# New orders for an attention-plus-MLP kernel, with fewer dummy matmuls in its first batch

One core of one Trainium2 chip. The metric is device time of one execution in microseconds (us), the slowest core's; here there is one. Dies and slow dies do not matter.

## The reference

Nyström attention on 8 batches of 8 heads, 576 tokens, head dimension 64, with 32 landmarks, followed by an MLP with squared ReLU.

```python
A  = sm(q, k_lm); Bm = sm(q_lm, k_lm); C = sm(q_lm, k)     # sm: scaled scores, softmax
Z  = Bm.T / (norm1(Bm) * norminf(Bm) + 1e-6)
for _ in range(6):
    Z = 2 * Z - Z @ Bm @ Z                                  # Newton steps, 32x32 per head
attn = A @ Z @ C @ v
h = x @ w_in; r = max(h, 0); out = (r * r) @ w_out          # x: [4608, 512], d_ff 2048
```

## The kernel before

Each batch runs as named steps. A written list says in which order they are issued: HEAD for batch 0's attention, then one list per batch, which mixes that batch's MLP (`h`: four matmuls of 288 columns and a relu; `s`: the square) with the next batch's attention and with output matmuls (a number n: n matmuls of 512 columns). Each engine follows the list in order; it waits only where its next instruction's inputs are missing.

```python
HEAD = (
    "w:16 ck tk1 mk w:1:256 w:1:256 ek1d w:1:256 w:1 tk0 tt w:1 w:1 cq0 cq1 ek0a mq tq0 tq1 "
    # ... cut ...
    "jl at:0 ea0d ea1a ct w:1:256 nu w:1:256 g:0 gl1d fv w:1 gf1d w:1 gf0a az gl0d"
)
```

`w:n:width` is n dummy matmuls, which keep TensorE busy and compute nothing:

```python
def warm(n, width=512):
    z = bds[1].rearrange("p a b c -> p (a b c)")
    for _ in range(n):
        nc.tensor.matmul(idle[:, 0:width], lhsT=z[:, 0:P], rhs=z[:, 0:width], start=True, stop=True)
```

The other steps of the head that matter here: `ck`, `cq0`, `cq1` reorder k and the two halves of q as they arrive; `tk`, `tq` transpose on TensorE and `ek`, `eq` copy the result out (last letter: `d` VectorE, `a` ScalarE); `mk`, `mq` are the segment means; `ls`, `ib`, `if` lead to EY, the start of the inverse; `jo` is one joint Newton step (four in all), `jl`, `nu`, `fv` the last ones; `sum`, `rec`, `row` normalise the score rows of A on VectorE; `cv`, `cr` are C times v and C's column sums; `az` gives AZ, after which the MLP of batch 0 can begin.

```python
def joint_step(old, diagonal):
    nv = products(diagonal, lambda qd: ...)           # 8 matmuls of 32x32 blocks on TensorE
    new = newt.tile([P, 2, 2, M], BF16, tag="EY", name="EY")
    last = twice_less(new, old, nv)                   # one VectorE instruction: 2*old - nv
    return new, stationary(new[:, :, 0, :], "ED"), last
```

The softmax here doesn't subtract the row's maximum and nothing guards it: scores larger than these inputs give would overflow.

Of the kernel before, what the change touches and what calls it, by code (L numbers as in the profile page):

```python
# [9 lines left out]
P = 128  # L10
# [23 lines left out]
DMA_C = 9  # L34
COMPACT = 1
HEAD = (
    "w:16 ck tk1 mk w:1:256 w:1:256 ek1d w:1:256 w:1 tk0 tt w:1 w:1 cq0 cq1 ek0a mq tq0 tq1 "
    "lm w:1 et w:1:256 w:1 eq0a w:1:256 tl eq1d ls sum:0:4:5 w:1 ib w:1 w:1:256 sq1 w:1:256 "
    "if sk1 sum:1:2:5 w:1:256 w:1 sum:1:0:2 jo w:1:256 w:1:256 rec:1 w:1:256 row:1:0:3 "
    "row:1:3:5 w:1:256 sk0 w:1 sq0 jo w:1:256 w:1:256 w:1 w:1:256 sum:0:2:4 sum:0:0:2 w:1 jo "  # L40
    "rec:0 cv:0 cv:1 w:1:256 w:1:256 row:0:3:5 cr jo w:1:256 row:0:0:3 w:1:256 at:1 cba w:1 "
    "jl at:0 ea0d ea1a ct w:1:256 nu w:1:256 g:0 gl1d fv w:1 gf1d w:1 gf0a az gl0d"
)
LOADS = "w10 v0 w00 q1 w01 w11 o0 o1 o2 o3 v1"
PLANS = [
    (
        "pk h g:1 tt h pq h s tk1 s h s h tq1 s tk0 h h mk s s mq tq0 h lm s g:2 g:3 ls sk0 s h "
        "h ib 1 h 1 s if tl h jo 1 sq0 s 1 jo s s 1 h jo 1 sq1 1 jl h 1 nu h s s h nn 2 sk1 nu s "
        "1 s 8 as0 1 ar0 as1 2 ar1 5 nn1 cv 4 wt at0 2 gg0 2 at1 2 gg1 1"
    ),  # L50
    (
        "2 pk 1 h h 1 mk pq s mq 1 s h tq0 lm h ls h tt tq1 3 tl 1 s 1 h ib 1 s if s sq1 2 s h "
        "jo 1 as1 sq0 1 h h s 1 as0 tk1 1 jo 1 s 4 tk0 2 jo 1 h 1 s h 1 pk+ 1 jl ar1 h sk0 1 s 1 "
        "s nu h s 1 sk1 s h h nn s cv nu h 3 nn1 at1 s 3 s wt 3 ar0 2 gg0 3 at0 1 gg1 pq+"
    ),
    (
        "5 mk h 1 h mq s 2 h 5 lm s 2 ls 1 sk1 2 ib 3 h h s sk0 s if 1 s h 2 h 1 jo s h tl 3 jo "
        "1 s 2 h jo 1 s 2 h 3 s sq0 s 1 jl pk+ 4 sq1 2 as0 nu 3 h 1 nn 2 as1 1 pq+ 1 nu 1 h 1 "
        "ar1 h 1 s s h 1 nn1 cv 1 h 2 ar0 1 s wt h 1 at0 2 gg1 1 s at1 1 s 2 gg0 1 s"
    ),  # L60
    (
        "mk 2 h 1 mq 7 h 2 s lm s 1 ls 1 h sq1 1 h h 1 ib 1 s if sk1 1 s h s 2 h jo 1 s 1 h s 1 "
        "jo 2 h 1 pk+ jo 1 tl s h 2 jl as1 sq0 1 s h 1 s h nu s 1 h sk0 s 1 ar1 4 as0 nn 1 ar0 2 "
        "h 3 cv 2 s h nu 4 s nn1 1 at1 1 h wt 2 s 3 s gg1 1 at0 4 gg0 4 pq+"
    ),
    (
        "2 mk h 2 mq 4 h lm 1 h 1 s ls 1 sk0 s ib s 3 h h if 3 tl s 2 h h s 1 s jo 2 h h 1 jo s "
        "1 sq0 s 2 h 1 jo 5 s 10 jl pk+ s 3 sq1 h nu 1 h 1 h 3 as0 sk1 s 1 h 1 as1 ar1 5 s nn cv "
        "nu pq+ 4 s 2 nn1 ar0 h s 4 wt h 2 at0 s 1 gg0 2 s 1 at1 1 gg1 2"
    ),  # L70
    (
        "3 mk mq 3 h lm 3 h h ls 1 s 1 s ib 2 sq1 h 2 if 1 sq0 3 jo h 1 sk0 s jo 2 s h jo tl 4 "
        "as1 1 h 1 jl s sk1 h 3 pk+ s 4 nu h 1 s 2 s 1 s 4 as0 h 1 ar1 nn s 2 ar0 h cv h nu h s "
        "1 s 1 nn1 h 2 h pq+ s wt h 2 at1 2 gg0 at0 5 s 3 s s gg1"
    ),
    (
        "mk 1 mq 3 h s lm 1 h 3 ls 2 h s 1 ib 2 h 1 if sq1 s h 1 s 3 sq0 2 s h 2 s 2 jo h tl 3 "
        "jo 1 h h as0 jo 3 s h 1 s jl 1 s sk1 4 nu 2 as1 h nn 1 h 1 sk0 2 ar0 nu 1 s s 3 h h 1 "
        "cv 2 nn1 s h s 1 at0 1 wt h 2 s 1 ar1 gg0 1 at1 2 s 1 gg1 4 s"
    ),  # L80
    (
        "h 7 h 6 s 1 h 6 h 1 s 2 h s 2 h 6 s 13 h 2 s 2 h 1 s 1 s 5 s h 3 h 1 s s h 11 s 1 h s 8 "
        "h 1 h 1 h 1 s 4 s h 2 s s"
    ),
]

# [2 lines left out]
def kernel(  # L89
# [9 lines left out]
    nc = tc.nc  # L99
# [27 lines left out]
        nc.vector.memzero(ect[:])  # L127
        ects.append(ect)

    behind, gate = [], []  # L130

    def load(dst, src, queue=nc.gpsimd):
        with tc.issue_after(behind[0].ins) if behind else nullcontext():
            d = queue.dma_start(dst, src)  # L134
        if gate:
            tc.add_manual_dep(
                d.ins, gate.pop().ins.name,
                mybir.DependencyInfo(mybir.DependencyClass.Sync, mybir.DependencyReason.DATA),
                reason="q first")
        if queue is nc.gpsimd:  # L140
            behind[:] = [d]
        return d

    def k_row(b):
        return TAIL if b % 2 == 0 else 0

    def q_row(b):
        return TAIL - k_row(b)
# [12 lines left out]
    def load_qk(b: int, X: dict):  # L161

        X["qkt"] = loads.tile([P, H, D], BF16, tag="qkt", name="qkt")

        def tails():
            for src, r0 in ((k, k_row(b)), (q, q_row(b))):
                load(X["qkt"][r0:r0 + TAIL, :, :],
                     src[b, :, NC4 * P:S, :].rearrange("h p d -> p h d"))

        if b > 0:  # L170
            tails()
        for nm, src in (("k", k), ("q", q)):
            if b < 3:
                X[nm + "raw"] = staged(b, nm)
            else:
                X[nm + "raw"] = loads.tile([P, H, NC4, D], BF16, tag="raw", name="raw")
            parts = ((0, H // 2), (H // 2, H)) if b == 0 and nm == "q" else ((0, H),)
            for lo, hi in parts:
                one = load(
                    X[nm + "raw"][:, lo:hi, :, :],  # L180
                    src[b, lo:hi, 0:NC4 * P, :].rearrange("h (p c) d -> p h c d", c=NC4),
                    nc.sync if b == 0 and nm == "k" else nc.gpsimd)
                if b > 0 and nm + "turn" in loaded[b - 1]:
                    tc.add_manual_dep(
                        one.ins, loaded[b - 1][nm + "turn"].ins.name,
                        mybir.DependencyInfo(mybir.DependencyClass.Sync,
                                             mybir.DependencyReason.DATA),
                        reason="behind the turning of the batch before")
            if b == 0 and nm == "k":
                tails()  # L190

# [9 lines left out]

    loaded = {b: {} for b in range(B)}
    load_qk(0, loaded[0])

    def band(t, pattern, base, mult):
# [28 lines left out]
    for i in range(2):  # L234
        ct = const.tile([P, 2, NC4 + 1, P], BF16, name="ct%d" % i)
# [1 line left out]
        cts.append(ct)  # L237
    nc.vector.tensor_copy(seg[:, NC4 + 2, :], seg[:, NC4, :])

    def load_rest(after):  # L240

        def w_in(i, j):
            load(
                w_in_bf[64 * i:64 * i + 64, :, 1024 * j:1024 * j + 1024],
                moe_w_in[256 * i:256 * i + 256, 1024 * j:1024 * j + 1024].rearrange(
                    "(j d) f -> d j f", d=D),
            )

        def w_out(j):
            load(  # L250
                w_out_bf[:, 4 * j:4 * j + 4, :],
                moe_w_out[512 * j:512 * j + 512, :].rearrange("(ft fp) c -> fp ft c", fp=P),
            )

        behind[:] = [masked]
        for x in LOADS.split():
            i = int(x[1])
            if x[0] == "w":
                w_in(i, int(x[2]))
            elif x[0] == "o":  # L260
                w_out(i)
            else:
                (load_v if x[0] == "v" else load_qk)(i, loaded[i])

    turn = [0]
# [32 lines left out]
    def attention(b: int, R: dict):  # L298

        X = loaded[b]  # L300
        BD = bds[b % 2]
        ect = ects[b % 2]
        first = b == 0
# [193 lines left out]
        ct = cts[b % 2] if b >= DMA_C else None  # L497
        c0 = b % 2
        at = NC4 * (1 - c0)
# [10 lines left out]
        an = attn.tile([P, 2, NC4 + 1, P], BF16, tag="an", bufs=1, name="an")  # L510
        AT = attn.tile([P, 2, (NC4 + 1) * P], BF16, tag="AT", name="AT")
# [55 lines left out]
        one, two = slice(0, 1), slice(1, 2)  # L567
# [20 lines left out]

        def a_transposed(i):
            if b >= DMA_A:  # L590
                nc.sync.dma_start_transpose(AT[:, i, :].rearrange("p (c t) -> p c t", t=P),
                                            an[:, i, :, :].rearrange("p c x -> p (c x)"))
                return
            tps = ntile([P, (NC4 + 1) * P], BF16, placed=b > 0)
            for c in range(NC4 + 1):
                nc.tensor.transpose(tps[:, c * P:c * P + P], an[:, i, c, :], ident_bf[:])  # L596
            o = TAIL * c0
            return AT[:, i, o:o + S], tps[:, o:o + S]
# [42 lines left out]
        act, dve = nc.scalar.copy, nc.vector.tensor_copy  # L641
# [67 lines left out]
        def head_step(token):  # L709
            st = X["state"]  # L710
            name, *args = token.split(":")
            i = int(name[2]) if len(name) > 2 and name[2].isdigit() else 0
            n = [int(x) for x in args if x.isdigit()]
            on = [x for x in args if not x.isdigit()]
            if name == "ck":
                raw = natural(0, "k")
                dve(X["k"][:, 0:2], raw[:, 0:2])
                load_rest(act(X["k"][:, 2:4], raw[:, 2:4]))
                st["qraw"] = natural(0, "q")
                X["tT"] = attn.tile([P, NPAIR, P], BF16, tag="tT", name="tT")  # L720
            elif name[:2] == "cq":
# [62 lines left out]
            elif name == "az":  # L784
                AZ = attn.tile([P, 2, (NC4 + 1) * P], BF16, tag="AT", name="AZ")
                az = [psum.tile([P, 2, 512], F32, tag="h", bufs=2, name="az") for j in range(2)]
# [187 lines left out]
```

## Time and profile before

| | kernel before |
|---|---|
| time, median (range) of its first four runs | 263.62 us (263.31 to 264.01) |
| profiled span | 262.1 us |
| head: start to the first MLP matmul (first h) | 23.51 us |
| body: first h to TensorE's last matmul | 234.96 us |
| after it, until the end | 3.65 us |
| dummies between the steps of the head | 14 of 512 columns, 21 of 256 |

I call the stretch to the first h the head and the rest the body, and read busy time of the engines by stretch for both. The columns are the stretch, its length, then busy us and number of instructions of TensorE, its weight loads, VectorE, ScalarE and GpSimd, then the clock, the DMA share and GB/s.

```profile
12.30:23.50 11.20, 10.71 (x221) 6.89 (x218) 9.58 (x34) 6.51 (x15) 5.24 (x8) 1.00 1.49 197
23.50:258.50 235.00, 234.22 (x2574) 141.49 (x2574) 159.46 (x431) 147.35 (x257) 28.85 (x37) 1.00 0.81 127
```

In the body TensorE is busy 234.2 of 235.0 us. In the head it looks just as busy (10.71 of 11.20 us), but of the head's array time from 6.7 us on, 5.3 us are dummies, about 4.1 us of them in this stretch.

### The profile page before, as it was taken

Reading aid. Unit: us, or ns where it says so; the run is one execution under the profiler, and the core shown is the slowest. Engines: PE = TensorE matmul, PEld = TensorE weight load, DVE = VectorE, ACT = ScalarE, POOL = GpSimd, SP = SyncE. Lnnn points to the kernel's source line nnn. Section 1 sums busy time; section 2 is a strip of 40 time slices with the busy share of each in tenths; the row PEclk is TensorE's granted clock in tenths of the full one; section 3 lists DMA queues with packets and bytes.
Section 4 is the critical chain, followed back from the end, with each engine's and each line's share of the span. In section 5 each row is a group of like instructions: output and inputs, shape, how many; then the busy total and the mean of one; then the engine's idle time right before and its main releaser. Section 6 shows DMA issues by size and latency. Waiting matters only on the chain.

```text
span 262.1 us, 6993 instructions
## 1 busy us (share of the span) xinstructions
PE 254.6 (97%) x2894; PEld 154.1 (59%) x2894; DVE 176.8 (67%) x488; ACT 158.4 (60%) x278; POOL 45.2 (17%) x70
## 2 busy tenths in 40 slices
PE   7899999999999999999999999999999999999994
PEld 2674765476746655666566565566566655555453
DVE  5798777789985888699757587689776783232000
ACT  1556985478755856687567556775777664364210
POOL 8934234120010503301005010600000000000000
PEclk9999999999999999999999999999999999999999
DMA  8999999999549999995759979699401112112122
GB/s 185 201 194 205 208 205 189 204 210 90 116 48 207 126 173 214 160 170 109 144 103 95 204 149 181 92 197 216 102 22 40 43 43 80 40 44 80 40 80 80
DMA packets 69791, 34.65 MB, mean 132 GB/s; under 512 B 37376, under 2 KB 64256, under 8 KB 69760
## 3 DMA queue, kind: packets, MB, share of 16 engines
q0 software_dynamic: 39808, 17.83, 56.8%
q1 hardware_dynamic: 24704, 7.08, 16.0%
q10 hardware_dynamic: 5248, 9.31, 11.0%
q8 instruction: 22, 0.36, 0.6%
q14 instruction: 9, 0.07, 0.1%
HBM read 36.70 MB, written 9.44 MB: 176 GB/s over the span
## 4 chain that ended last, share of the span: by engine, by line
PE 91%; DVE 4%; DMA 2%; ACT 1%; issue 1%; DVEq 0%
PE ops L851 25%; PE h L822 24%; PE n L851 22%; PE g L805 3%; PE n L530 3%; DMA stage<-in_k_dram 2%; PE n L342 2%; PE n L414 2%; PE n L596 2%; PE idle L295 2%; PE n L614 1%; PE n L313 1%; PE n L629 1%; ACT r L826 1%; PE n L558 1%; DVE gT L827 1%
## 5 line engine op out<-in xcount | busy, mean ns | idle before, releaser
L826 ACT ACTIVATE r<-h 128x576 bf16<-128x576 f32 x128 | 81.3, 652 | 45.9 <-PE h L822 34.1
L851 PE MATMUL ops<-w_out_bf,gT 128*128 128x512 bf16 (+1 forms) x320 | 81.7, 368 | 0.0
L851 PEld LDWEIGHTS <-gT 128*128 128x128 bf16 x592 | 53.2, 98 | 38.7 <-issue 4.2
L851 PE MATMUL n<-w_out_bf,gT 128*128 128x512 bf16 x272 | 74.5, 379 | 0.0
L827 DVE TENSOR_TENSOR gT<-r 128x576 bf16<-128x576 bf16 x128 | 54.9, 448 | 27.2 <-ACT r L826 27.0
L822 PE MATMUL h<-AT,G 128*128 128x288 bf16 x448 | 71.0, 286 | 0.0
L822 PEld LDWEIGHTS <-G 128*128 128x128 bf16 x512 | 47.7, 97 | 24.2 <-ACT AZ L795 0.7
L703 DVE CAST G<-g 128x1024 bf16<-128x1024 f32 x14 | 17.1, 1224 | 5.4 <-PE g L805 5.4
L862 ACT COPY o_sb<-ops 128x512 f32<-128x512 f32 (+1 forms) x19 | 10.9, 574 | 14.5 <-PE ops L851 14.5
L862 ACT COPY o_sb<-n 128x512 f32<-128x512 f32 x17 | 10.0, 587 | 12.9 <-PE n L851 12.8
L703 ACT CAST G<-g 128x1024 bf16<-128x1024 f32 x14 | 14.2, 1015 | 4.5 <-PE g L805 4.5
L295 PE MATMUL idle<-bd 128*128 128x512 bf16 (+1 forms) x51 | 13.3, 377 | 1.5 <-DVE bd L117 1.5
L530 PEld LDWEIGHTS <-T 128*128 128x128 bf16 x256 | 11.3, 98 | 4.2 <-issue 0.6
L134 POOL DMA_DIRECT2D raw<-in_k_dram x5 | 4.5, 891 | 52.2 <-DVE gT L827 25.5
L572 DVE TENSOR_REDUCE ra<-EA 128x20 f32<-128x640 f32 (+3 forms) x19 | 13.2, 703 | 0.3 <-ACT EA L560 0.3
L584 DVE TENSOR_TENSOR an<-EA,rra 128x640 bf16<-128x640 f32 (+2 forms) x18 | 13.2, 737 | 0.2
L530 PE MATMUL n<-bd,T 128*128 128x64 bf16 x256 | 12.7, 193 | 0.0
L535 ACT ACTIVATE EA<-n 128x512 f32<-128x512 f32 x16 | 9.6, 598 | 3.3 <-PE n L530 3.2
L535 ACT ACTIVATE EC<-n 128x512 bf16<-128x512 f32 x16 | 9.5, 596 | 3.0 <-PE n L530 1.6
L134 POOL DMA_DIRECT2D raw<-in_q_dram x5 | 4.4, 884 | 38.2 <-DVE rc L445 17.1
L414 PEld LDWEIGHTS <-ED 128*128 128x128 bf16 x72 | 6.8, 98 | 6.5 <-DVE EY L453 0.9
L822 PE MATMUL h<-AZ,G 128*128 128x288 bf16 x64 | 10.0, 286 | 0.6 <-DVE AZ L795 0.4
(144 smaller groups left out, 287.2 us busy)
## 6 DMA issues: line engine op xcount, KB each, us to landing
out_dram<-o_sb ACTq DMA_DIRECT2D x31, 256.0 KB, 3.4
vm<-in_v_dram POOLq DMA_DIRECT2D x8, 512.0 KB, 10.8
raw<-in_k_dram POOLq DMA_DIRECT2D x5, 512.0 KB, 6.4
raw<-in_q_dram POOLq DMA_DIRECT2D x5, 512.0 KB, 6.2
w_in_bf<-in_moe_w_in_dram POOLq DMA_DIRECT2D x4, 512.0 KB, 12.1
w_out_bf<-in_moe_w_out_dram POOLq DMA_DIRECT2D x4, 512.0 KB, 17.0
out_dram<-o_sb ACTq DMA_DIRECT2D x9, 128.0 KB, 2.4
stage<-in_k_dram SPq DMA_DIRECT2D x1, 1024.0 KB, 5.9
```

The source lines that it names most:

```text
L295: nc.tensor.matmul(idle[:, 0:width], lhsT=z[:, 0:P], rhs=z[:, 0:width], start=True, stop=True)
L414: nc.tensor.matmul(res[a:a + w, qd, :], lhsT=diagonal[a:a + w, qd, :], rhs=moving(qd)[a:a + w], start=True, stop=True)
L530: nc.tensor.matmul(sc[:, c, j, :, :], lhsT=X[nm + "T"][:, c, p, :], rhs=BD[:, 1 if nm == "q" else 0, p, 0:64], start=True, stop=True)
L535: nc.scalar.activation(dst, sc.rearrange("p c j i m -> p c (j i m)"), AF.Exp, scale=SCALE)
L572: nc.vector.reduce_sum(ra[:, quads, lo:hi, :], EA[:, quads, lo:hi, :].rearrange("p q c (h m) -> p q c h m", m=M), axis=AX.X)
L584: on.tensor_tensor(an[:, i, lo:hi, :].rearrange("p c (h m) -> p c h m", m=M), EA[:, i, lo:hi, :].rearrange("p c (h m) -> p c h m", m=M), r ...
L703: (act, dve)[n % 2](G[:, :, n * 512:n * 512 + 512], gg[:])
L822: nc.tensor.matmul(h[:, j, 0:HALF], lhsT=G[:, qd, f * P:(f + 1) * P], rhs=AT[:, qd, a0 + j * HALF:a0 + (j + 1) * HALF], start=(qd == 0), s ...
L826: nc.scalar.activation(r.rearrange("p (j t) -> p j t", j=2), h[:, :, 0:HALF], AF.Relu)
L827: return lambda: nc.vector.tensor_tensor(gT[:, f, o:o + S], r[:], r[:], ALU.mult)
L851: nc.tensor.matmul(ops, lhsT=gT[:, f, t * P:t * P + P], rhs=w_out_bf[:, f, i * n:i * n + n], start=(f == 0), stop=(f == NF - 1))
L862: nc.scalar.copy(o_h, ops)
```

## The change

The intent: the orders of all lists come from a new search, and the head has fewer dummies (9 of 512 columns and 4 of 256 instead of 14 and 21; the 16 at the very start stay). In the head six copies also change engine: the copies of the transposed k and q swap VectorE and ScalarE, and two copies of G (`gl`) go from VectorE to ScalarE. Where I say "order" of the head below, these are included. The rest of the diff is inert: a list that was never filled is removed, and a new dependence concerns a path that is switched off.

```diff
 HEAD = (
-    "w:16 ck tk1 mk w:1:256 w:1:256 ek1d w:1:256 w:1 tk0 tt w:1 w:1 cq0 cq1 ek0a mq tq0 tq1 "
-    "lm w:1 et w:1:256 w:1 eq0a w:1:256 tl eq1d ls sum:0:4:5 w:1 ib w:1 w:1:256 sq1 w:1:256 "
-    "if sk1 sum:1:2:5 w:1:256 w:1 sum:1:0:2 jo w:1:256 w:1:256 rec:1 w:1:256 row:1:0:3 "
-    "row:1:3:5 w:1:256 sk0 w:1 sq0 jo w:1:256 w:1:256 w:1 w:1:256 sum:0:2:4 sum:0:0:2 w:1 jo "
-    "rec:0 cv:0 cv:1 w:1:256 w:1:256 row:0:3:5 cr jo w:1:256 row:0:0:3 w:1:256 at:1 cba w:1 "
-    "jl at:0 ea0d ea1a ct w:1:256 nu w:1:256 g:0 gl1d fv w:1 gf1d w:1 gf0a az gl0d"
+    "w:16 ck tk0 w:1 ek0d w:1:256 tk1 w:1 cq0 mk cq1 tt w:1 et ek1a mq tq0 lm eq0d tl ls tq1 "
+    "w:1 ib eq1a w:1:256 if sq1 sum:0:4:5 jo sq0 sum:1:2:5 sum:1:0:2 sk1 jo rec:1 sum:0:2:4 "
+    "w:1:256 sk0 sum:0:0:2 w:1 w:1:256 jo cv:0 cv:1 row:1:0:3 jo rec:0 cr row:1:3:5 cba "
+    "row:0:3:5 w:1 w:1 row:0:0:3 ct at:1 jl w:1 ea1a at:0 nu ea0d fv g:0 gf1d gf0a az gl0a "
+    "w:1 gl1a"
 )
 PLANS = [
-        "pk h g:1 tt h pq h s tk1 s h s h tq1 s tk0 h h mk s s mq tq0 h lm s g:2 g:3 ls sk0 s h "
+        "pk h tt s h g:1 pq s tk1 h h tk0 tq1 h mk s mq h s s tq0 lm ls h h s sq1 g:2 g:3 ib s h "
     # ... cut: the rest of this list and seven more, all reordered ...
```

## The prediction

> **What bounds the kernel now.** I read the page's first two parts first, to see which engine fills the span.

> ```profile
> span 262.1 us, 6993 instructions
> PE 254.6 (97%) x2894; PEld 154.1 (59%) x2894; DVE 176.8 (67%) x488; ACT 158.4 (60%) x278; POOL 45.2 (17%) x70
> ...
> PEclk9999999999999999999999999999999999999999
> ```

> TensorE is busy 97% at the full clock. That is an average, so I cut the span at the first MLP matmul of batch 0 (the h of 128x288), which the timeline of PE puts at 23.51 us. Two regimes come out.

> From 23.5 us on ("body"), the order of the steps hardly matters as long as PE has something to do. From the starts of successive matmuls in the trace, a 512-wide one occupies the array for 215.7 ns, a 288-wide one 122.3 ns, a 128-wide one 56 ns and the small ones 25 to 28 ns. The view of groups by shape gives the counts:

> ```profile
> L851 PE MATMUL ops<-w_out_bf,gT 128*128 128x512 bf16 x288 | 78.2, 379 | 0.0
> L851 PE MATMUL n<-w_out_bf,gT 128*128 128x512 bf16 x272 | 74.5, 379 | 0.0
> L822 PE MATMUL h<-AT,G 128*128 128x288 bf16 x448 | 71.0, 286 | 0.0
> ```

> 560 x 215.7 ns is 120.8 us; 512 of the h (448, and 64 more of batch 0) x 122.3 is 62.6 us. With all smaller ones, added up in the same way, the body's matmul stream is 227.0 us. It runs from 23.5 to 258.3 us, 234.8 us. So only 7.8 us of the body are gaps in which the array has no next matmul: 2.4 us before 40 us, 1.0 between 40 and 60, and 4.4 in all the rest. Of the 7.8 us, 2.0 are the 0.1 us or so that 17 groups of the eight packed w_in products (g, L805) lose, mostly the second of a pair. After 258.3 us there are 3.8 us of drain, copy and last store.

> Before 23.5 us ("head"), batch 0's attention is a chain of short dependent steps, and dummy matmuls (tile idle, L295) fill PE between them. The groups of the stretch from 6.7 to 23.5 us by shape:

> ```profile
> L295 PE MATMUL idle<-bd 128*128 128x512 bf16 x15 | 5.3, 379 | 0.0
> L295 PE MATMUL idle<-bd 128*128 128x256 bf16 x21 | 4.5, 274 | 0.0
> ```

> One of the 15 is the tail of the 16 that run while k is loading; 14 belong to the steps. By array time, 14 x 0.216 + 21 x 0.109 is 5.3 us, against 8.6 us of real matmuls in this head. The chain that ended last names them as 37% of the stretch 12 to 24 us. I do not take this at face value: the chain walks back along PE whenever PE was not idle, and a dummy makes it not idle. The question is what would have come instead, so I looked at VectorE in the timeline:

> ```profile
> 14.39 0.17 DVE L445 RECIPROCAL rc<-n 128x2 f32<-128x2 f32 x1
> 14.96 0.22 DVE L451 TENSOR_TENSOR EY<-n,rc 128x64 bf16<-128x64 f32 x1 [0.41 <-PE n L414]
> 15.11 0.21 DVE L453 TENSOR_TENSOR EY<-BB,rc 128x64 bf16<-128x64 f32 x1
> 15.31 0.88 DVE L572 TENSOR_REDUCE ra<-EA 128x12 f32<-128x384 f32 x2
> 16.11 0.28 DVE L419 SCALAR_TENSOR_TENSOR EY<-EY,n 128x128 bf16<-128x128 bf16 x1
> ...
> 21.77 0.48 DVE L644 TENSOR_SCALAR G<-n,rc 128x256 bf16<-128x256 f32 x1 [0.59 <-PE n L805]
> ```

> The reader is to see the brackets: the idle time before an instruction. From 12.3 to 23.5 us VectorE is busy 9.58 of 11.2 us (busy time by windows). The Newton step's combination (L419) waits its turn behind sums and row scalings (L572, L584) of about 0.4 to 0.9 us, not behind PE. Only 0.41, 0.21 and 0.59 us are VectorE waiting for PE after 13 us, and earlier 0.69, 0.51 and 0.15 us.

> [...] Here the clock stayed at full share through the dummies; no run yet shows it without them. [...]

> **The change part by part.** The functions compute the same; the removed gate list was never filled, and the new dependence concerns a turning by DMA that is switched off (its threshold is batch 9 of 8). What is left is the order.

> 1. Dummies. Counting the tokens: 14 of 512 and 21 of 256 become 9 and 4; the 16 at the start stay. Removed array time is 5 x 0.216 + 17 x 0.109 = 2.9 us. This is an upper limit for their own worth, since where VectorE was late they covered idle time.

> 2. The new order of the head, walked by hand with the durations and latencies above (about 0.03 us from a matmul's end to a copy's start, 0.06 to 0.18 us back):
> - k's first half is transposed first; it needs only VectorE's cast (ends 7.50), not ScalarE's (7.77). PE starts at about 7.55 instead of 7.82.
> - k's evacuation by VectorE goes to 8.3 (was 9.30), q's two reorderings to 8.9 and 9.9 (were 9.9 and 10.24). The second can't go earlier: q's second half lands at about 10.0 at the latest.
> - q's means then are ready at about 11.1 (was 11.42), landmark scores at 11.5 (was 12.12). The softmax starts when VectorE has evacuated one q transpose, at about 12.1 (was 12.93): 0.8 us ahead.
> - The inverse's first step: the old order put a row sum (0.29 us) and three dummies in it. EY is done at about 14.1 (was 15.32): 1.2 us ahead.
> - Then come four joint steps with the same five sums, two reciprocals and four row scalings, in another order. This part is VectorE's own work and stays its length. The fourth joint step ends at about 17.7 instead of 19.65 because the row scalings move behind it; these then end at 19.2 instead of 20.12. The last joint step's result comes at 19.3 (was 20.33), its transpose at 19.6.
> - One of G's evacuations (0.48 us) leaves VectorE before AZ: the last two pieces go to ScalarE behind it. The last v is at 20.8 (was 22.38), az's products at about 21.0, AZ at 22.0 (was 23.37).

> So the first h comes at about 22.1 instead of 23.5: 1.4 us. A hand walk misses queueing, and every miss is late, so I book 1.1 us, with 0.4 to 1.7 as its range.

> 3. The plans. Matmul counts are equal (16 h per batch, 592 output matmuls); nothing is saved but gaps. The first 16.5 us of the body hold 2.4 us of gaps while only h, g and small steps are at hand. The new plan 0 has the same eight h before g:2, but one more score group there, and starts its output matmuls at the same place. Two places won't shift: g:2 and g:3 need the last w_in part, which lands at 29.7 us (they ran at 31.77; I expect 29.9 to 31), and the 13th output matmul needs the last w_out part, 39.9 us. Ahead of AZ, two evacuations on ScalarE delay the first relu by about 0.3 us. Later plans interleave differently at gaps of about 0.6 us per 20 us. I book 0.6 us of the removable 5.8, range -0.6 to +1.5.

> Sum: 1.1 + 0.6 = 1.7 us; 263.7 - 1.7 = 262.0 us.

> **The rivals.**
> (a) Dummies were the true path: the whole 2.9 us comes back, and plans add 1 to 1.5 us: about 259.5. For it: the chain's 37%. Against: VectorE's 86% in that stretch and its short brackets. I give it little.
> (b) The clock. With the steps' dummies down from 5.3 to 2.4 us, the array is occupied about 11 of 14.5 us, 0.75 (it was 0.82 to 0.92 in any 3.4 us between 7 and 23.5). [...]
> (c) The head's gain is given back: PE gets to plan 0 earlier, but batch 1's inputs (k at 22.1, q at 24.7 us), w_in at 29.7 and w_out at 39.9 come at the pace of the loads, some 200 GB/s, that compute doesn't move. Then PE waits in plan 0 instead, and the time stays at about 263.4. For it: the loads fill the DMA until 40 us. Against: in the old trace none of these transfers was waited for, with 2.1 us to spare at g:2.
> (d) The new plans are worse on the chip than in the search: a gap of 0.5 us like the one at 169 us, several times over, costs 1 to 2 us: 264 to 265.

> **Range and chances.** Faster by 2% needs under 258.5 us, 5.2 us. Even rival (a)'s 2.9 us needs another 2.3 us of the body's 5.8 us of removable gaps. Slower by 2% needs 269, more than the clock rival and bad plans together. The range spans from most of (a) to (c): 260.3 to 263.7. Chances 0.05, 0.93, 0.02.

> **What would show it.** The first h at 21.8 to 22.8 us, fewer L419 delays, the VectorE brackets small: step 2 right. The first h at 20.6 or before: (a). PEclk below 9 before 25 us: (b). PE waiting for DMA of k, q, w_in or w_out before 42 us: (c). Gaps in the body, counted as above, at 7.2 us would confirm step 3; over 9 us is (d). The prediction is wrong if the time leaves 260.3 to 263.7, above all if the body gained more than 2 us, since I hold its order to be nearly exhausted.

That the clock would stay full was my estimate. That I count starts rests on the trace: of the 560 matmuls of 512 columns in the kernel before, 517 have the next start 215 to 217 ns after their own, while a row lasts 379 ns in the mean.

## The result

262.74 us, median of four runs (262.51 to 262.79), against 263.62 us: ratio 0.9964, interval 0.9947 to 0.9981. Ratios here are the mean time of one kernel's fast runs over that of the other's fast runs of the same rounds, so not quite the ratio of the medians that I quote. The 0.9 us are inside the predicted range and within 2%.

The page after, its first parts:

```profile
span 261.0 us, 6950 instructions
PE 252.8 (97%) x2872; PEld 151.8 (58%) x2872; DVE 175.9 (67%) x486; ACT 158.9 (61%) x280; POOL 45.7 (18%) x70
...
PEclk9999999999999999999999999999999999999999
```

At this distance nothing has changed. Busy time by stretch, cut at the new first h (22.48 us):

```profile
12.30:22.50 10.20, 8.50 (x197) 5.04 (x195) 8.32 (x31) 6.13 (x15) 4.50 (x8) 1.00 1.49 196
22.50:257.40 234.90, 234.25 (x2574) 140.90 (x2574) 159.25 (x430) 147.97 (x260) 30.16 (x38) 1.00 0.79 128
```

The body is 234.88 us (was 234.96), with gaps of 7.7 us (were 7.8). The whole gain is the first h, 1.04 us earlier. TensorE in the late head is less busy than before (83% against 96%), and that part is still shorter. The chain that ended last, between 12 us and the first h, first of the kernel before (the stretch to 24 us), then of the new one:

```profile
by line: PE idle L295 37.0%; PE n L414 9.3%; PE n L530 8.7%; PE n L596 5.5%; issue 5.0%; PE n L429 5.0%; PE h L822 4.4%; DVE AZ L795 3.9%; PE az L790 3.8%; PE n L614 3.5%; PE n L805 3.5%; PE tps L313 2.8%; PE n L629 1.9%; PE n L558 1.9%; DV
```

```profile
by line: PE n L412 11.7%; ACT EA L533 11.3%; issue 10.5%; ACT EC L533 10.4%; DVE T L729 6.6%; ACT AZ L795 6.0%; PE n L595 5.5%; PE n L528 5.0%; PE n L613 4.7%; ACT G L642 4.4%; PE n L805 3.9%; DVE btc L422 3.2%; PE idle L293 3.1%; DVE EY L4
```

The dummies fall from 37% to 3.1% of it. "issue", time in which an engine waits for nothing that the profile shows, rises to 10.5%. VectorE's timeline says where to look for that (start, duration, instruction; in brackets the idle time before it). The L417 lines are the four joint steps:

```profile
13.91 0.21 DVE L451 TENSOR_TENSOR EY<-BB,rc 128x64 bf16<-128x64 f32 x1
...
14.48 0.29 DVE L417 SCALAR_TENSOR_TENSOR EY<-EY,n 128x128 bf16<-128x128 bf16 x1 [0.15 <-PE n L412]
...
15.63 0.28 DVE L417 SCALAR_TENSOR_TENSOR EY<-EY,n 128x128 bf16<-128x128 bf16 x1
...
16.61 0.28 DVE L417 SCALAR_TENSOR_TENSOR EY<-EY,n 128x128 bf16<-128x128 bf16 x1
16.81 0.55 DVE L582 TENSOR_TENSOR an<-EA,rra 128x384 bf16<-128x384 f32 x1
18.15 0.29 DVE L417 SCALAR_TENSOR_TENSOR EY<-EY,n 128x128 bf16<-128x128 bf16 x1 [0.79 <-PE n L412]
```

EY is done at 14.12 us, 1.2 us earlier than before, as the prediction had it (14.1). Steps one to three follow well. The fourth is late: VectorE waits 0.79 us for TensorE, and TensorE's own timeline at that place is odd:

```profile
16.12 0.24 PE L412 MATMUL n<-EY 32*32 32x64 bf16 x8
...
16.97 0.23 PE L412 MATMUL n<-EY 32*32 32x64 bf16 x5
17.90 0.20 PE L412 MATMUL n<-EY 32*32 32x64 bf16 x3 [0.70 <-issue]
18.04 0.25 PE L628 MATMUL n<-ones_bf,EC 128*128 128x1 bf16 x4
```

The eight matmuls of one step are cut in two. Their starts are 0.89 us apart (17.01 and 17.90). The sixth waits for no semaphore and the clock is full. Without this pause the first h would have been nearer 21.6 us (an estimate: 22.48 less 0.89).

### The profile page after: what moved, and what is told of

The parts are those of the page before. It is cut to its first block, busy times and chain, and to the rows that moved or that the text cites. A ratio compares the mean times of both kernels' runs of the same rounds, so it can differ in the third digit from the quotient of the medians.

```text
span 261.0 us, 6950 instructions
## 1 busy us (share of the span) xinstructions
PE 252.8 (97%) x2872; PEld 151.8 (58%) x2872; DVE 175.9 (67%) x486; ACT 158.9 (61%) x280; POOL 45.7 (18%) x70
## 4 chain that ended last, share of the span: by engine, by line
PE 90%; ACT 3%; DMA 2%; DVE 1%; issue 1%; POOL 1%; POOLq 0%
PE ops L851 26%; PE h L822 24%; PE n L851 23%; PE g L805 3%; PE n L528 3%; DMA stage<-in_q_dram 2%; PE n L340 2%; PE n L412 2%; PE n L595 2%; PE n L613 1%; PE n L311 1%; PE n L628 1%; ACT G L642 1%; ACT EA L533 1%; PE n L556 1%
## 5 line engine op out<-in xcount | busy, mean ns | idle before, releaser
L851 PE MATMUL ops<-w_out_bf,gT 128*128 128x512 bf16 (+1 forms) x320 | 81.1, 368 | 0.0
L851 PEld LDWEIGHTS <-gT 128*128 128x128 bf16 x592 | 53.1, 97 | 40.9 <-issue 5.1
L851 PE MATMUL n<-w_out_bf,gT 128*128 128x512 bf16 x272 | 74.5, 379 | 0.0
L822 PE MATMUL h<-AT,G 128*128 128x288 bf16 x448 | 71.2, 286 | 0.0
L827 DVE TENSOR_TENSOR gT<-r 128x576 bf16<-128x576 bf16 x128 | 55.1, 445 | 21.6 <-ACT r L826 21.3
L822 PEld LDWEIGHTS <-G 128*128 128x128 bf16 x512 | 47.0, 97 | 21.4 <-ACT AZ L795 0.4
L528 PEld LDWEIGHTS <-T 128*128 128x128 bf16 x256 | 11.2, 98 | 4.5 <-DVE T L661 0.4
L293 PE MATMUL idle<-bd 128*128 128x512 bf16 (+1 forms) x29 | 9.5, 443 | 1.5 <-DVE bd L116 1.5
L822 PE MATMUL h<-AZ,G 128*128 128x288 bf16 x64 | 10.2, 286 | 0.1
L417 DVE SCALAR_TENSOR_TENSOR EY<-EY,n 128x128 bf16<-128x128 bf16 x25 | 7.1, 283 | 3.9 <-PE n L412 3.8
L340 PEld LDWEIGHTS <-nat 128*128 128x128 bf16 x256 | 8.3, 96 | 2.5 <-DVE nat L723 0.3
## 6 DMA issues: line engine op xcount, KB each, us to landing
vm<-in_v_dram POOLq DMA_DIRECT2D x8, 512.0 KB, 11.6
```

The source lines that it names most:

```text
L340: nc.tensor.matmul(means[:, ti, p, :], lhsT=src.rearrange("p h d -> p (h d)"), rhs=seg[:, c + (ti if c == NC4 else 0), :], start=(n == 0 a ...
L528: nc.tensor.matmul(sc[:, c, j, :, :], lhsT=X[nm + "T"][:, c, p, :], rhs=BD[:, 1 if nm == "q" else 0, p, 0:64], start=True, stop=True)
L822: nc.tensor.matmul(h[:, j, 0:HALF], lhsT=G[:, qd, f * P:(f + 1) * P], rhs=AT[:, qd, a0 + j * HALF:a0 + (j + 1) * HALF], start=(qd == 0), s ...
L827: return lambda: nc.vector.tensor_tensor(gT[:, f, o:o + S], r[:], r[:], ALU.mult)
L851: nc.tensor.matmul(ops, lhsT=gT[:, f, t * P:t * P + P], rhs=w_out_bf[:, f, i * n:i * n + n], start=(f == 0), stop=(f == NF - 1))
```

## The experiments

Two theories of the gain stood against each other. *Order*: the head was bound by VectorE and its chain, and the new order shortens it. *Dummies*: the removed dummies had been on the path. Beside them the *instruction* theory of the pause and the *clock* rival. All kernels gave correct results. The table has all runs. "h - k" is the first h after VectorE's or ScalarE's first cast of k, which takes out that k lands between 6.3 and 6.9 us from run to run; "EY - k" is the end of EY counted the same way; "EY to h" is the rest. "Lowest clock" is the lowest mean granted clock of its timed executions (the profiled one among them). Everything after the third column but the last is from the profiled execution, one for each kernel.

| kernel | median (range), us | ratio to before, interval | first h | EY - k | EY to h | h - k | body | lowest clock |
|---|---|---|---|---|---|---|---|---|
| before | 263.62 (263.31 to 264.01) | | 23.51 | 8.60 | 8.19 | 16.79 | 234.96 | 0.997 (42 later runs) |
| after | 262.74 (262.51 to 262.79) | 0.9964, 0.9947 to 0.9981 | 22.48 | 7.31 | 8.35 | 15.66 | 234.88 | 0.998 |
| after_again | 262.96 (262.61 to 265.55) | 0.9996, 0.9966 to 1.0026 | 22.18 | 7.66 | 7.90 | 15.56 | 235.22 | 0.984 |
| a_head | 262.80 (262.21 to 264.84) | 0.9978, 0.9944 to 1.0013 | 22.21 | 7.78 | 7.93 | 15.71 | 234.77 | 0.984 |
| b_plans | 263.23 (263.01 to 263.97) | 0.9986, 0.9963 to 1.0009 | 23.21 | 8.51 | 8.19 | 16.70 | 234.97 | 0.999 |
| b_few | 262.89 (262.70 to 264.60) | 0.9979, 0.9951 to 1.0006 | 22.91 | 8.31 | 7.89 | 16.20 | 234.60 | 0.993 |
| a_moredum | 263.71 (263.45 to 264.07) | 1.0010, 0.9998 to 1.0023 | 23.50 | 8.09 | 9.04 | 17.14 | 234.96 | 0.998 |
| a_rows | 262.53 (262.00 to 262.84) | 0.9953, 0.9929 to 0.9977 | 21.79 | 7.88 | 7.46 | 15.34 | 235.14 | 0.997 |
| a_rows2 (same) | 262.25 (261.79 to 263.59) | 0.9964, 0.9943 to 0.9984 | 21.68 | 7.65 | 7.45 | 15.10 | 235.07 | 0.998 |
| a_w9 | 262.92 (261.91 to 266.17) | 0.9970, 0.9954 to 0.9987 | 22.20 | 7.73 | 7.98 | 15.71 | 235.06 | 0.987 |
| b_rows | 263.40 (263.13 to 263.65) | 0.9998, 0.9985 to 1.0012 | 23.14 | 8.51 | 8.19 | 16.70 | 234.52 | 1.000 |
| a_nodum | 264.34 (263.90 to 267.14) | 1.0049, 1.0016 to 1.0081 | 23.15 | 7.82 | 8.76 | 16.58 | 236.56 | 0.973 |
| b_nodum | 265.13 (264.69 to 265.37) | 1.0060, 1.0048 to 1.0072 | 23.85 | 8.23 | 8.77 | 17.00 | 235.89 | 0.979 |
| a_rowsnd | 264.25 (263.67 to 264.87) | 1.0027, 1.0013 to 1.0041 | 23.52 | 8.30 | 8.93 | 17.23 | 235.52 | 0.971 |

One thing stands out before any single run. Wherever the clock stayed full in the profiled execution, the body is 234.5 to 235.2 us, whatever the order. So the experiments are about the head.

**Head and plans apart.** a_head is the new kernel with the old plans; b_plans is the old head with the new plans.

```diff
 # a_head, from the new kernel: PLANS is that of the kernel before
 # b_plans, from the kernel before: PLANS is that of the new kernel
```

> The new head with the old plans. If the gain is the head's alone, as the two traces say (first h 23.51 to 22.48 us, gaps in the body 7.81 against 7.72 us), this is 0.9 us under the kernel before, at 262.7 us, with the first h at 22.4 to 22.6 us. If the plans carry half of the gain, it is at 263.2. The rival that an earlier head is given back to the loads says 263.5: the first h early and the body's gaps up by 1 us. The pause of 0.89 us inside the fourth joint step (fifth and sixth of its eight matmuls, none of which waits for a semaphore) should appear again at the same place if it is tied to the row of PE's program; if it is an accident of one execution it is absent.

> The old head with the new plans. Head theory: the first h at 23.5 us as before and a time within 0.3 us of the kernel before, 263.3 to 263.9. If the plans matter: 263.0 or less, or over 264.0 if they fit only the new head.

The new head alone has h - k at 15.71 us, as the full change (15.66), and the median of the full change within 0.1 us. The new plans alone leave the body at 234.97 us, and 263.23 us is not to be told from the kernel before (the interval contains 1). So the plans are worth nothing that these runs can resolve; the head carries the gain. a_head's own interval (0.9944 to 1.0013) contains 1 too, because two of its six executions had a lower clock (below), so this rests on the first h and the body of the profiled executions. Its first h came at 22.21 us, before the 22.4 to 22.6 that I gave, mostly because k landed 0.3 us earlier. The rival that an early head is given back to the loads falls: the body did not grow. And the pause is back, at the same row:

```profile
17.13 0.23 PE L412 MATMUL n<-EY 32*32 32x64 bf16 x5
17.64 0.20 PE L412 MATMUL n<-EY 32*32 32x64 bf16 x3 [0.28 <-issue]
```

This is a_head's TensorE timeline. TensorE came to the step 0.16 us later than in the first trace, the block was ready a little earlier, and the pause is 0.46 us between starts. It is no accident of one execution.

**Dummies and order apart.** b_few takes the same number of dummies out of the old order; a_moredum puts them back into the new one, at steps like those where the old order had them. The placing is mine, not the search's.

```diff
 # b_few, from the kernel before: 5 of the 14 "w:1" and 17 of the 21 "w:1:256" deleted
-    "... tt w:1 w:1 cq0 cq1 ... lm w:1 et w:1:256 w:1 eq0a w:1:256 tl ..."
+    "... tt w:1 cq0 cq1 ... lm w:1 et eq0a tl ..."
 # a_moredum, from the new kernel: 5 "w:1" and 17 "w:1:256" added
-    "... jo cv:0 cv:1 row:1:0:3 jo rec:0 cr ... row:0:0:3 ct at:1 jl w:1 ..."
+    "... jo cv:0 cv:1 w:1:256 row:1:0:3 jo rec:0 w:1:256 cr ... row:0:0:3 w:1:256 w:1:256 ct at:1 w:1 jl w:1 ..."
```

> The kernel before with 9 and 4 dummy matmuls between the steps instead of 14 and 21, the order untouched: 2.9 us of array time less, 44 rows of PE's program less. VectorE theory: the first h moves by 0.2 to 0.6 us, the time is 263.1 to 263.5. Dummy rival: it moves by 2 us or more, time 261.6 or less. Instruction theory (a block of 256 rows of PE's program can be used at the earliest 6.2 us after PE has entered the block before it): 44 rows fewer put the block's first row later in the work, and a pause without a semaphore of 0.2 to 0.9 us appears at row 449, in the stretch from 17 to 18.5 us, which takes part of the gain.

> The new order with as many dummies between the steps as the kernel before (14 of 512 and 21 of 256): what the order is worth alone. Dummy rival: the first h returns to 23.3 us or later and the time to 263.5. Order theory: EY stays near 14.1 to 14.7 us, since q's second half (10.0 to 10.3 us) sets it and not the dummies; after it dummies cost up to 0.6 us, but 26 to 44 more rows ahead also take the block's first row out of the fourth joint step, so the pause is gone or shorter; first h 22.2 to 22.9 us, time 262.6 to 263.1, about that of the new kernel.

b_few: h - k is 16.20 us against 16.70 to 16.79, so in the old order the 22 dummies cost 0.5 to 0.6 us, at the upper end of what I expected from the order theory and far from the 2 us of the dummy rival. Its time of 262.89 us lies under the 263.1 to 263.5 that I gave. The pause that I expected in it did not show: TensorE came to row 449 at 18.13 us, 1.46 us after the packet's end, just when it was to be had.

a_moredum refutes my expectation. In the new order the same 22 dummies cost 1.4 to 1.6 us (17.14 against 15.56 to 15.71), and the time is back at 263.71 us. EY came at 14.46 us, inside what I had written, but the rest took 9.04 us instead of 7.9 to 8.4. The chain of this run from 14 to 24 us:

```profile
by line: PE idle L293 35.9%; PE n L412 14.1%; PE n L528 13.2%; ACT G L642 7.5%; ACT AZ L795 7.0%; PE n L613 6.6%; PE n L595 5.6%; issue 4.1%; PE az L790 3.8%; PE n L805 3.4%; PE n L628 2.3%; PE n L757 1.2%
```

Here the dummies' share in the chain is in part real: TensorE reaches its steps late. But the pause, which I expected gone or shorter, is in this chain too. It stands before row 449 again, now inside the matmuls of C times v ahead of the fourth joint step, with 0.56 us between starts (17.36 and 17.92):

```profile
17.92 0.23 PE L613 MATMUL n<-vm,EC 128*32 128x64 bf16 x5 [0.37 <-issue]
```

The new kernel has a pause of 0.46 to 0.89 us as well, so the 1.4 to 1.6 us compare two paused heads. The kernel before has none. So the order alone shows no gain, with my placing of the dummies: 17.14 us with the pause and about 16.6 without it (an estimate by subtraction), against 16.70 to 16.79. The dummies alone are worth 0.5 to 0.6 us, and both together 1.1 us. Against the new order without a pause (15.10 and 15.34 us, next) the dummies cost about 1.2 to 1.5 us by the same estimate. As I read the timelines, the new order is one that can use a free TensorE, and the old one leaves VectorE busy with row scalings when TensorE is ready; no run tests this.

**The pause.** a_rows moves the whole head 52 rows down TensorE's program without adding time: 42 narrow dummies at the start, while k is loading, instead of 16 wide ones. a_rows2 repeats it on one chip beside the new kernel. a_w9 goes 14 rows up, with fewer starting dummies. b_rows is the control: the shift of a_rows in the kernel before, which had no pause.

```diff
 # a_rows, a_rows2 (new kernel) and b_rows (kernel before)
-    "w:16 ck ..."
+    "w:16:256 w:26:128 ck ..."
 # a_w9 (new kernel)
-    "w:16 ck ..."
+    "w:9 ck ..."
```

> The new kernel with its 16 starting dummies of 512 columns replaced by 16 of 256 and 26 of 128, which take about the same 5 us (an estimate from the starts: 427 ns per 512 columns cold, 56 ns per 128 warm), so that every later instruction stands 52 rows further down PE's program. Instruction theory: the block then begins 26 matmuls earlier in the work, is asked for at about 10.1 us instead of 11.6 and is there at about 16.3 us, before PE needs it at 16.6; the pause of 0.89 us is gone, the first h comes 0.4 to 0.8 us earlier than 22.48, time 262.0 to 262.3. Rival (the pause comes from something else, such as ScalarE or a PSUM bank in the fourth joint step): the pause stays at the fourth joint step, time 262.7.

Its starts, from the kernel before: the starting dummies of 512 columns start 426 to 427 ns apart from 1.92 to 4.91 us and 215 to 216 ns apart from 5.18 us on; later matmuls of 128 columns mostly start 55 to 56 ns apart.

> The new kernel with 9 instead of 16 starting dummies, so that every later instruction stands 14 rows higher in PE's program; the head behind it is untouched. Instruction theory: the block's first row, which was the load of the sixth matmul of the fourth joint step, is now the load of about the fifth of the ten column sums that follow that step. The pause of 0.4 to 0.9 us moves there with it, the fourth joint step runs undivided, and its result comes 0.7 us or so after the third's instead of 1.1 to 1.5; the first h 0.3 to 0.8 us earlier, time 262.1 to 262.5. Rival (the pause belongs to the joint step): it stays at the step, the time at 262.7. [...]

> The new kernel unchanged, to stand beside the next two on the same chip: 262.6 to 262.8 us, the first h 15.6 to 15.8 us after VectorE's first cast of k, EY finished 4.1 us after the second reordering of q has begun, and a pause of 0.4 to 0.9 us without a semaphore inside the fourth joint step.

> The shift of 52 rows once more, beside the new kernel on the same chip. Instruction theory: no pause, EY to first h 7.4 to 7.6 us against 7.9 to 8.4 in the new kernel, time 0.2 to 0.8 us under it. If the gain of the first such run was chance, the two times agree within 0.1 us.

> Control of the shift: the kernel before with the same 16 + 26 narrower starting dummies, 52 rows more ahead of everything. It has no pause in its chain to lose (its block was ready about when PE came to it), so by the instruction theory its first h stays 16.6 to 16.9 us after the first cast of k and its time within 0.3 us of the kernel before. If the narrower starting dummies help by themselves (an earlier end, a warmer clock), it gains 0.4 us or more as the new kernel did.

a_w9's TensorE timeline:

```profile
17.05 0.24 PE L412 MATMUL n<-EY 32*32 32x64 bf16 x8
17.22 0.25 PE L628 MATMUL n<-ones_bf,EC 128*128 128x1 bf16 x4
17.86 0.18 PE L628 MATMUL n<-ones_bf,ect 128*128 128x1 bf16 x1 [0.39 <-issue]
```

The joint step is whole, and the pause (0.55 us between starts) stands before the fifth column sum, 14 rows further on in the work. But the first h gained nothing against a_head and after_again (h - k 15.71 us): TensorE's next steps stand behind the sums, and the last joint result comes at 19.67 us, where a_rows2 has it at 19.15. To move the pause out of the step is not enough; it has to go. a_rows2, on TensorE and then on VectorE:

```profile
17.06 0.24 PE L412 MATMUL n<-EY 32*32 32x64 bf16 x8
17.23 0.25 PE L628 MATMUL n<-ones_bf,EC 128*128 128x1 bf16 x4
```

```profile
16.70 0.28 DVE L417 SCALAR_TENSOR_TENSOR EY<-EY,n 128x128 bf16<-128x128 bf16 x1
...
17.36 0.28 DVE L417 SCALAR_TENSOR_TENSOR EY<-EY,n 128x128 bf16<-128x128 bf16 x1
```

No pause in a_rows2; its fourth joint step follows the third by 0.66 us instead of 1.54. EY to h is 7.46 and 7.45 us in the two runs, against 7.90 to 8.35 with the pause in the step. The packets confirm the reading:

```
run          earlier block entered   packet        row 449 runs   pause
after        11.64                   15.49-16.46   17.90          0.89
after_again  11.77                   15.20-16.17   17.60          0.47
a_w9         12.11                   15.62-16.60   17.86          0.55
a_moredum    11.66                   15.49-16.44   17.92          0.56
a_rows2       9.92                   13.06-14.00   16.77          none
before       11.90                   15.71-16.66   18.28          none
```

(These six traces have all their matmuls; in a_head, a_rows, b_plans and b_few 43 to 45 are missing, so their rows are good to a few.) Where TensorE pauses, row 449 runs 1.3 to 1.5 us after the packet's end; where the packet came early, it doesn't pause. Every run of the new head with its rows not shifted down has a pause at this place, a_nodum too (0.28 us). The number of packets fits as well: by the theory blocks begin at row 193 and every 256 rows after it, and b_rows, the only program that goes beyond row 5825 (it has 5867 rows), has 23 packets, all others 22. What sets the delay of a packet stays open. It starts 3.1 to 3.9 us after the earlier block was entered in these heads. In the four that paused, row 449 ran 5.7 to 6.3 us after that entry: 3.4 to 3.9 us until the packet moved, 1.0 us for the packet, 1.3 to 1.5 us until the row ran. So the 6.2 us that b_few's expectation took as the earliest was not the earliest. Beyond 60 us, where the DMA load is lighter (112 to 113 GB/s, against 199 to 200 up to 40 us), it starts anywhere from 2.3 us before to 3.5 us after that row's start in the two kernels, so the request does not hang on the start that the trace shows, and that the load delays it is not shown. The control b_rows has h - k at 16.70 us and a ratio of 0.9998: the narrow dummies do nothing by themselves.

In time, the shift is worth 0.5 us in the profiled first h (22.18 to 21.68), and the medians of the two kernels on the same chip are 262.96 and 262.25 us. Their single runs overlap (262.61 to 265.55 and 261.79 to 263.59), and a_rows was only 0.2 us under the first four runs of the new kernel, so I call it ahead of both kernels by its medians and by the trace, by some tenths. a_rows's 262.53 us is outside the 262.0 to 262.3 that I gave; its first h is inside. a_w9's first h (22.20 us) fell just short of the range that I gave, and its time of 262.92 us is outside it: besides the pause, two of its six executions had clocks of 0.987 and 0.992 (the first, 266.17 us, counts as slow and is left out of the ratio; without it the median is 262.78 us, still outside). after_again's median of 262.96 us missed 262.6 to 262.8, and its EY came 4.39 us after the second reordering of q began, not 4.1; counted from the end of that instruction the rule holds better (below).

**The clock.** The last three have no dummies between the steps at all: a_nodum in the new order, b_nodum in the old one, a_rowsnd in the new order with shifted rows.

```diff
 # a_nodum (new kernel), b_nodum (kernel before): every "w:" token but the first deleted
 # a_rowsnd (new kernel): the same, and
-    "w:16 ck ..."
+    "w:12:256 w:40:128 ck ..."
```

> The new kernel without any dummy between the steps. Clock rival: the granted clock falls below 1 somewhere between 8 and 24 us and the time rises to 263.5 or more. If the array's real work of the head is enough to keep the clock, the time is not above the new kernel's. Instruction theory: the pause lies behind the fourth joint step here too (18 rows fewer ahead of it), so the first h is 0.3 to 0.8 us earlier than in the new kernel, time 262.0 to 262.4. If dummies were all that mattered, 2.4 us of array time less would give 260.4.

> The kernel before without any dummy between the steps: 5.3 us of array time less. VectorE theory: the first h comes at 22.4 to 22.9 us (it was 22.9 with 9 and 4 dummies left), time 262.5 to 262.9. Dummy rival: the first h at 20 us or earlier, time under 261. Clock rival: the clock falls, time over 263.5. An order of its own worth is shown if the new kernel without dummies is still ahead of this one.

> The new order without dummies between the steps, and with 52 narrower starting dummies (12 of 256 columns and 40 of 128) in place of the 16, so that the block of PE's program begins early and no pause falls into the chain. If VectorE bounds what is left, the first h comes at 21.5 to 21.9 us and the time is 262.0 to 262.4, no better than with the shift alone; if dummies still cost, up to 1 us less. The body from the first h to PE's last matmul should be 234.6 to 235.2 us here as in all six traces so far.

All three are slower than the kernel before, as the clock rival had it; the times that I gave the other theories are missed by 1.9 us or more. a_rowsnd's body (235.52 us) left the range that I gave, too. Busy time by stretch, first a_nodum, then the new kernel in the same stretches; the third column from the end is the clock:

```profile
13.30:16.70 3.40, 2.65 (x66) 1.77 (x65) 3.02 (x13) 2.96 (x5) 1.33 (x3) 1.00 1.40 202
16.70:27.00 10.30, 9.05 (x145) 5.39 (x146) 7.46 (x20) 5.28 (x13) 3.94 (x6) 0.50 1.40 199
```

```profile
13.30:16.70 3.40, 2.97 (x88) 1.99 (x91) 3.03 (x14) 2.74 (x5) 1.36 (x3) 1.00 1.40 204
16.70:27.00 10.30, 8.59 (x168) 5.25 (x158) 7.73 (x21) 6.51 (x15) 4.32 (x6) 1.00 1.40 199
```

The clock halves at 16.75 us (share 0.50) and comes back at 26.99, 10.24 us later. In b_nodum it is halved from 16.88 to 27.12, again 10.24 us, in a_rowsnd from 11.90 to 25.55, 13.65 us. The two lengths differ by 3.41 us and are three and four times that. While it was halved, matmul rows filled 9.05 of 10.30 us in a_nodum. TensorE was not idle all through such a stretch: in a_nodum its rows filled 2.65 of 3.40 us before the fall. Counted from the starts of the matmuls (each at most until the next one's start), its array was occupied 36% of the 3.41 us before the fall in a_nodum, 35% in b_nodum and 45% in a_rowsnd. In the profiled heads that kept the clock, the poorest stretch of that length, cut at the clock's own edges, had 45 to 67%, the new kernel's 47%. The counts are good to a few per cent, so there is no sharp line in them, only that the new head is close to what lost the clock. In all 18 timed executions without dummies the mean clock was 0.971 to 0.994. The cost shows in the head and behind it: a row of the h matmuls lasts 440 ns in the mean from 23 to 27 us of a_nodum, against 286 ns over the whole of the kernel before, and a_nodum's body is 236.56 us.

This may also explain the stray runs of the new kernel. Of 16 executions with the new head and its 16 starting dummies (after, after_again, a_head), three had a mean clock of 0.984 to 0.991 and took 263.94, 264.84 and 265.55 us; the other 13 had 0.998 or more. b_few, with as few dummies, had one of six (0.993, 264.60 us). Of 42 executions of the kernel before in the later rounds, none was below 0.997. None of those three was profiled, so where their clock fell is not shown; a half clock in the head for 1.4 to 2.5 times 3.41 us fits in size (an estimate: 1 less 0.984 to 0.991 is 0.009 to 0.016, which times some 263 us over the half that is lost makes 4.7 to 8.4 us). They count as fast runs, and one alone moves after_again's ratio to 0.9996.

## Why the prediction was right, and where not

1. *Dummies (step 1).* I took 2.9 us as an upper limit and gave them no figure of their own, since VectorE looked like the bound. Removing them in the old order gave 0.5 to 0.6 us. But putting them back in the new one cost 1.4 to 1.6 us (1.2 to 1.5, estimated, against the new order without its pause). The rejection of rival (a), that the chain's 37% was real, was too strong: in the new order the dummies are on the path.

2. *The head (step 2).* Right in size: 1.1 us booked, 1.04 measured. The walk itself was right up to the third joint step: EY at 14.1 (14.12), softmax start 12.1 (12.05). It put the fourth joint step at 17.7 (18.44) and the first h at 22.1 (22.48). What the reserve for "queueing" met was mostly one thing, the pause at row 449. In a_rows2, without it, the fourth step ends at 17.64 and the first h comes at 21.68. That 1.1 us fits 1.04 is therefore in part luck: the walk's own 1.4 us is what the shifted heads reach (1.4 to 1.7 us by h - k), and the 0.3 us taken off stood for something that I had not seen. The limit ahead of EY was q's second half, as the walk said: VectorE's second reordering ends at 10.47 us in the new kernel and 10.56 to 10.73 us in a_rows, a_rows2, a_head, a_w9, a_nodum and after_again, and in all seven EY ends 3.65 to 3.66 us after it. I attributed the head's end to VectorE; of the gain of h - k (1.13 us), EY - k holds 1.29 us and EY to h -0.16, that is, the part which I thought VectorE-bound kept its length because of the pause and shortens to 7.45 us without it.

3. *The plans (step 3).* This term failed. I booked 0.6 us and named 7.2 us of gaps as its proof. The gaps were 7.7, and the new plans alone left the body at 234.97 us. The difference between the 1.7 us predicted and the 0.9 measured is this term and 0.1 to 0.2 us of scatter.

4. *The rivals.* (b), the clock: right for the profiled execution. In a_nodum the clock fell after 3.41 us in which the array was sparsely occupied (36%), not idle. I also had the occupancy too high, with 0.82 to 0.92 in any 3.4 us of the old head and 0.75 for the new one. Counted as above, stretches of 3.4 us between 7.6 and 23.5 us had 56 to 91% in the old head and 43 to 90% in the new: the average over the whole head hid the poor stretches. (c), given back to the loads: refuted, the body is constant. (d), worse plans: refuted.

## What to carry to other kernels

Before tuning an order, measure whether the saturated part of the kernel reacts to order at all; here 235 us did not, and all of the gain sat in the 23 us before it. Filler work that keeps a clock up has two prices: here 22 of 35 dummies cost 0.5 us in one order and 1.2 us or more in another, with the 13 that were left three of 16 executions showed a lower mean clock, and with none the clock fell in every profiled one, 0.3 to 0.6% behind the kernel before. Where an engine pauses between two instructions that wait for nothing, look at the traffic of its program, and move the pause by adding rows where time is free (here 0.28 to 0.89 us, gone with 52 rows more).
